# Fourier mixing and a gated FFN on one core: the odd item of the third stage goes ninth, and the first batch's loads, stores and conversions are put in another order

## The chip, the cores and the metric

The kernel runs on one core of a Trainium2 chip. The metric is the device time of one execution in microseconds (us). Before the change it is 2895.74 us, the median of three runs (2893.91 to 2896.57). A core has TensorE (PE, matmuls), VectorE (DVE), ScalarE (ACT), GpSimd (POOL) and SyncE (SP). In this kernel SP does nothing but issue DMA transfers; POOL issues DMA transfers too, and ACT issues the stores of the third stage. Each engine works through its own list of instructions strictly in the order in which they were written, so an instruction that waits holds up all that stand behind it on the same engine.

## The reference

Eight batches of 3072 rows by 256 channels go through a spectral mixing layer: a real Fourier transform along the rows, a complex 256x256 product at each frequency with a bias, a soft threshold, and the transform back. The result goes row by row through a feed-forward network of width 2048 with the activation h·tanh(softplus(h)). Weights of the network come as 64-bit floats.

```python
X = np.fft.rfft(x, axis=1)
Yr = Xr @ w_r - Xi @ w_i + b_r
Yi = Xr @ w_i + Xi @ w_r + b_i
Yr = np.sign(Yr) * np.maximum(np.abs(Yr) - lam, 0.0)      # the same for Yi
y = np.fft.irfft(Yr + 1j * Yi, n=3072, axis=1)
h = y @ w_in
out = (h * np.tanh(np.where(h > 20.0, h, np.log1p(np.exp(h))))) @ w_out
```

## The kernel before

Every product is done with operands that are split in a rounded high part ("hi") and the remainder ("lo"); three matmuls (hi·hi, lo·hi, hi·lo) stand for one. The split costs one instruction for hi (ACT's L197 in the first batch, DVE's L195 later) and one on DVE for lo (L198).

**The four stages of a batch.** The transform of 3072 points is factored. Stage one (`item_a`, 7 items, PE line L361, in the chain's segment 0) loads x and does 24-point transforms; its results go to a DRAM scratch s1 (store L380 in the first batch). Stage two (segment 1) alternates 12 blocks `item_b` (L427 and L430 in the first batch; the load of s1 is L398, the twiddle table "tt" is loaded at L406) with 12 mixing items `item_m` (L543 in the first batch), which add the bias, apply the threshold (DVE lines L481 to L483, output tile y) and store y to the scratch s3 (L572: four stores of 32 rows per block; the odd block 11 uses L562, L564 and L586). Stage three (`item_c`, PE L634) gathers lines of s3 by strided DMA loads (L612), and stores to the scratch s2 from ACT's queue (L637). It has 13 items: items 0 to 11 take 4 loads each, the odd item 12, which has the leftover frequencies, takes 6, and stands first. Stage four (`item_f`, PE L675 and L676, load of s2 at L652, its table vt at L657 from c_v in the first batch and at L659 from v_scr later) gives a piece of the rows y that the network reads. Two of its items make one chunk of 512 rows; a batch has six chunks.

**The network.** For each chunk, 16 steps of `ffn1` (L757: 6 matmuls of 128x512, then the activation on ACT at L762), `split_g` (L771, L772) and `ffn2` (L788: 12 matmuls of 128x256 per step).

**What sets the order.** The program is written out step by step by Python generators. `run_chain` walks through a batch's four segments; it issues the loads of the first `ahead_n` items of a segment before the segment starts, and then one item's loads ahead of each item (`ahead`). For the first batch `ahead_n` is 6 and nothing else fills PE, so the four stages run one after the other. After that, the network's steps of batch b run, and each step draws one piece of the chain of batch b+1 (`gen`, ahead_n 3) or of the next chunk's stage-four item (`extra`), whichever is there; `extra` goes first. So PE has, in each step, 6 + 12 matmuls of the network and one piece of a chain, and the loads of both chains stand in the one list of SP.

**The weight conversions.** The 16 pieces ("jobs") of the 64-bit weights are loaded from POOL (L261, tile raw, 512 KB each) and turned into float32 hi and lo by nine instructions each: seven on DVE (L269 to L285; the last comes with ACT's L287) and two (L291, L293) that finish the job inside the next one. `aux_steps(n)` writes the next n of these instructions. PACE gives how many of them follow one piece of segment 0, 1, 2 or 3 of the first batch; `on_seg` writes some between segments. At most 97 are written before the network starts; the rest follow in its first 19 steps. A raw tile is loaded as early as its place in POOL's list and its buffer allow.

**Queues.** In the first batch SP issues the loads of x, half of stage three's loads (those with g = 0) and all y stores; POOL issues tables, raw weights, bias, the constant uu of stage three, and the other half of stage three's loads (g = 1). From the second batch on, SP issues all loads and y stores. y tiles come from a pool of two (`p_z`), tables tt and vt from a pool of four (`p_t`).

Of the kernel before, what the change touches and what calls it, by code (L numbers as in the profile page):

```python
# [127 lines left out]
def fft_mix_ffn_kernel(ctx: ExitStack, tc: tile.TileContext, x, w_r, w_i, b_r, b_i, w_in, w_out,  # L128
                       c_fa, c_t0, c_t, c_u, c_v, out):
    nc = tc.nc  # L130
# [36 lines left out]
    started = [False]  # L167
# [128 lines left out]
    N_EARLY = 11  # L296
# [201 lines left out]
    def item_m(b, blk, src):  # L498
        it = Item()
# [56 lines left out]
        def store():  # L556
            y = it.y
            s3 = scratch(b)[1]
            yv = y.rearrange("p (s c) -> p s c", s=2)
            half = SEQ // 4  # L560
            if blk == 11:
                nc.sync.dma_start(out=s3[half, 1:2, :], in_=yv[0:1, 0, :])  # L562
                for h in range(2):
                    nc.sync.dma_start(  # L564
                        out=s3[0:half].rearrange("(i r) s c -> r i s c", r=12)[6 * h].rearrange("i s c -> i (s c)"),
                        in_=y[64 * h:64 * h + 64])
                return
            for e in range(2):
                for d in range(2):
                    r, x = (23 - blk, 1 - e) if d else (blk + 1, e)  # L570
                    rows = s3[(r % 2) * (half + 1):][0:half].rearrange("(i r) s c -> r i (s c)", r=24)
                    nc.sync.dma_start(out=rows[r // 2 + 12 * x], in_=y[64 * e + 32 * d:64 * e + 32 * d + 32])  # L572

        def nyq():
            xh, xl = src.x
# [68 lines left out]
    def item_f(b, nb):  # L644
        it = Item()
# [6 lines left out]
            nc.sync.dma_start(out=it.t, in_=s2[:, 2 * nb:2 * nb + 2, :].rearrange("q m c -> q (m c)"))  # L652

        def cload():
            it.v = p_t.tile([128, 2, 2, 128], F32R, tag="t", name="vt")
            if b == 0:
                nc.gpsimd.dma_start(out=it.v, in_=c_v[nb])  # L657
            else:
                nc.sync.dma_start(out=f32(it.v), in_=v_scr[nb])  # L659
# [30 lines left out]
    def chain(b):  # L690
        segs = [[item_a(b, p) for p in range(7)]]
        bm = []
        order = [11] + list(range(11))
        bs = [item_b(b, k) for k in order]
        for k in range(12):
            bm.append(bs[k])
            if k:
                bm.append(item_m(b, order[k - 1], bs[k - 1]))
        bm.append(item_m(b, order[11], bs[11]))
        segs.append(bm)  # L700
        segs.append([item_c(b, p) for p in (12, *range(12))])
        segs.append([item_f(b, 0), item_f(b, 1)])
        return segs

# [98 lines left out]
    with tc.manual_schedule():  # L803
# [9 lines left out]
        def aux_run():  # L813
            for n, job in enumerate(aux):
                aux_load(n + 1)
                for k, _ in enumerate(job.work(aux[n - 1] if n else None)):
                    if k == 5:
                        aux_load(n + (4 if n + 3 <= N_EARLY else 3))
                    yield
            yield from aux[-1].finish()  # L820

# [9 lines left out]
        def on_seg(k):  # L831
            if k == 1:
                setup_mix()
                aux_steps(4)
            elif k == 2:
                aux_steps(9)
            elif k == 3:
                aux_steps(8)

        PACE = (0.8, 0.9, 2.2, 2)  # L840
        first = chain(0)
        cnt = 0
        owed = 0.0
        for k in run_chain(first, ahead_n=6, ahead_a=3, cla=3, on_seg=on_seg):
            cnt += 1
            if cnt == 2:
                load_mix()
                aux_load(1)
            if cnt == 3:
                for it in first[1][:3]:  # L850
                    it.cload()
            if cnt == 5:
                load_bias()
                aux_load(2)
            if cnt == 9:
                aux_load(4)
            if cnt == 16:
                setup_u()
            if cnt > 5:
                owed += PACE[k]  # L860
            while owed >= 1:
                aux_steps(1)
# [71 lines left out]
```

## Time and profile before

| | before |
|---|---|
| median of three runs | 2895.74 us (2893.91 to 2896.57) |
| the profiled execution | 2898.05 us |
| its span, first to last instruction | 2896.3 us |
| mean granted TensorE clock | 0.981 |
| PE / DVE / ACT busy | 96% / 65% / 33% |
| DMA, mean over the span | 94 GB/s |

A row of the trace gives start, duration, engine, line, operation, output and input tiles and, in brackets, how long the engine had been idle before it and what ended that. "x4" at the end means four instructions that the answer merged; their time is the sum, so a merged row of a DMA queue runs from the first issue to the end of the last. The SP and POOL rows are issues; the transfer itself goes on after them. A row of stages gives, for a stretch of the span, the busy time of each engine with its number of instructions, the granted TensorE clock (1.00 is full), and the DMA's share and rate.

### The profile page before, as it was taken

How to read it: one execution, taken by the hardware profiler on the slowest of the kernel's cores; microseconds unless marked ns; L12 is line 12 of the kernel's file. 1: busy time of each engine (PE TensorE's matmuls, PEld its weight loads, DVE VectorE, ACT ScalarE, POOL GpSimd, SP SyncE). 2: the span in 40 equal slices, each digit the busy share in tenths (PEclk: the TensorE clock that was granted, in tenths of full speed). 3: DMA queues.
4: the chain of work that ended last, by engine and by line, in shares of the span. 5: the costliest groups of instructions: out<-in, count | busy, mean ns of one | idle time of the engine just before them, and what ended most of it. 6: DMA issues, size and time to landing. Idle time of an engine off the chain costs nothing.

```text
span 2896.3 us, 44966 instructions
## 1 busy us (share of the span) xinstructions
PE 2788.0 (96%) x17812; PEld 2506.2 (87%) x17812; DVE 1891.3 (65%) x3116; ACT 946.3 (33%) x1844; POOL 49.3 (2%) x90
## 2 busy tenths in 40 slices
PE   6779999999999999999999999999999999999999
PEld 4558988899898998889988899888989899889998
DVE  5888765767657775567755777567765777654443
ACT  3333333233333332333323333323333333232222
POOL 1210000000000000000000000000000000000000
PEclk9879999999999999999999999999999999999999
DMA  7654424232233322242233322432324232221010
GB/s 213 186 150 123 128 83 121 82 97 89 74 101 115 94 74 87 85 130 80 66 103 100 101 83 64 123 94 88 93 68 125 83 103 86 73 89 44 23 37 15
DMA packets 171528, 273.13 MB, mean 94 GB/s; under 512 B 22902, under 2 KB 67974, under 8 KB 170934
## 3 DMA queue, kind: packets, MB, share of 16 engines
q1 hardware_dynamic: 147958, 224.23, 25.7%
q10 hardware_dynamic: 13856, 25.17, 3.0%
q0 software_dynamic: 9504, 20.86, 2.6%
q8 instruction: 140, 2.29, 0.3%
q14 instruction: 70, 0.57, 0.1%
HBM read 169.49 MB, written 107.23 MB: 96 GB/s over the span
## 4 chain that ended last, share of the span: by engine, by line
PE 89%; DMA 4%; DVE 3%; SPq 2%; issue 1%; ACT 0%; POOL 0%; ACTq 0%; DVEq 0%; POOLq 0%
PE acc L788 37%; PE hp L757 35%; PE psp L526 4%; PE psa L361 2%; PE psc L634 2%; PE psk L507 2%; PE psf L675 2%; PE psb L442 2%; SPq L612 1%; PE psf L676 1%; PE psb L444 1%; DMA s<-y 1%; DMA lds<-s 1%; DVE lo L198 1%; DMA lds<-in_x_dram 0%
## 5 line engine op out<-in xcount | busy, mean ns | idle before, releaser
L788 PE MATMUL acc<-wout,gh 128*128 128x256 f32 x6144 | 1148.5, 285 | 0.0
L757 PE MATMUL hp<-yh,win 128*128 128x512 f32 x3072 | 1090.3, 395 | 5.0 <-ACT yh L684 4.3
L788 PEld LDWEIGHTS acc<-wout,gh 128*128 128x128 f32 x6144 | 977.7, 190 | 41.6 <-issue 6.0
L762 ACT ACTIVATE s<-hp 128x512 f32<-128x512 f32 x768 | 459.5, 598 | 1447.2 <-PE hp L757 1335.9
L788 PE MATMUL acc<-wout,gl 128*128 128x256 f32 x3072 | 871.1, 284 | 0.0
L757 PEld LDWEIGHTS hp<-yh,win 128*128 128x128 f32 x3072 | 582.1, 189 | 105.1 <-ACT yh L684 4.5
L757 PE MATMUL hp<-yl,win 128*128 128x512 f32 x1536 | 606.8, 395 | 0.0
L788 PEld LDWEIGHTS acc<-wout,gl 128*128 128x128 f32 x3072 | 583.8, 190 | 0.0
L772 DVE TENSOR_TENSOR gl<-s,gh 128x1024 fp32r<-128x1024 f32 x384 | 470.6, 1225 | 79.9 <-PE acc L788 42.6
L771 DVE CAST gh<-s 128x1024 fp32r<-128x1024 f32 x376 | 259.1, 689 | 332.8 <-ACT s L762 332.8
L757 PEld LDWEIGHTS hp<-yl,win 128*128 128x128 f32 x1536 | 291.0, 189 | 36.2 <-DVE yl L685 0.4
L198 DVE TENSOR_TENSOR lo<-ld,hi 120x512 fp32r<-120x512 f32 (+3 forms) x390 | 269.7, 692 | 28.9 <-ACT hi L197 16.3
L195 DVE CAST hi<-ld 120x512 fp32r<-120x512 f32 (+2 forms) x367 | 154.1, 420 | 82.6 <-DMA ld<-s 82.6
L679 DVE TENSOR_TENSOR eo<-psf,cor 128x256 f32<-128x256 f32 x192 | 77.3, 422 | 156.9 <-ACT cor L678 156.2
L634 PE MATMUL psc<-hi,uu 120*120 120x512 f32 (+1 forms) x224 | 93.0, 428 | 50.1 <-DVE hi L195 34.4
L526 PE MATMUL psp<-wmix,xh 128*128 128x256 f32 x672 | 133.0, 281 | 0.0
L361 PE MATMUL psa<-hi,fa 120*120 120x512 f32 (+1 forms) x224 | 97.2, 437 | 22.0 <-ACT hi L197 9.7
L526 PEld LDWEIGHTS psp<-wmix,xh 128*128 128x128 f32 x672 | 108.9, 188 | 3.7
L685 DVE TENSOR_TENSOR yl<-yt,yh 128x512 fp32r<-128x512 f32 x96 | 66.5, 693 | 67.0 <-ACT yh L684 67.0
L675 PE MATMUL psf<-vt,hi 128*128 128x256 f32 x384 | 95.3, 325 | 13.2 <-ACT hi L197 11.5
L684 ACT ACTIVATE yh<-yt 128x512 fp32r<-128x512 f32 x96 | 60.7, 632 | 139.4 <-DVE yt L682 139.4
L481 DVE TENSOR_TENSOR y<-psp,y 128x512 f32<-128x512 f32 x84 | 58.1, 691 | 70.3 <-PE psp L526 68.9
(107 smaller groups left out, 2419.4 us busy)
## 6 DMA issues: line engine op xcount, KB each, us to landing
ld<-s SPq DMA_DIRECT2D x185, 256.0 KB
out_dram<-ot SPq DMA_DIRECT2D x48, 512.0 KB
s<-y SPq DMA_DIRECT2D x352, 64.0 KB
ld<-in_x_dram SPq DMA_DIRECT2D x90, 240.0 KB
vt<-v_scr SPq DMA_DIRECT2D x84, 256.0 KB
s<-ev ACTq DMA_DIRECT2D x89, 240.0 KB
ld<-s SPq DMA_DIRECT2D x350, 60.0 KB
s<-eva SPq DMA_DIRECT2D x84, 240.0 KB
```

What stands on the lines that cost most here:

```text
L195: nc.vector.tensor_copy(out=hi, in_=src)
L198: nc.vector.tensor_tensor(out=lo, in0=src, in1=f32(hi), op=ALU.subtract)
L361: nc.tensor.matmul(out=ps[:K], lhsT=fa[:K, h, s, col:col + K], rhs=m[:K], start=n == 0, stop=n == 2)
L526: nc.tensor.matmul(out=it.ps[:, ri * 256:(ri + 1) * 256], lhsT=m[:, c, 130 - ri * 128:258 - ri * 128], rhs=wmix[:, c, s, 2 * ri, :], start ...
L634: nc.tensor.matmul(out=ps[:K, sl], lhsT=uu[:K, var, s, :K], rhs=m[:K, sl], start=n == 0, stop=n == 2)
L675: nc.tensor.matmul(out=ps[:, p], lhsT=it.hi[:, q:q + 128], rhs=it.v[:, p], start=True, stop=False)
L679: nc.vector.tensor_tensor(out=eo[:, c], in0=ps[:, :, 0], in1=cor, op=ALU.add)
L757: nc.tensor.matmul(out=hp, lhsT=win[:, k, s, f * 128:(f + 1) * 128], rhs=m[:, k, :], start=n == 0, stop=n == 5)
L762: nc.scalar.activation(out=s_t[t // 2][:, t % 2, :], in_=hp, func=ACTF.Mish)
L771: nc.vector.tensor_copy(out=gh, in_=s)
L772: nc.vector.tensor_tensor(out=gl, in0=s, in1=f32(gh), op=ALU.subtract)
L788: nc.tensor.matmul(out=p, lhsT=m[:, t % 2, o:o + 128], rhs=wout[:, f, s, :], start=f == 0 and h == 0 and n == 0, stop=last and h == 1 and ...
```

## The change

The change has two parts. The first acts in every batch: stage three's items run in the order 0 to 7, 12, 8 to 11, so the item with six loads stands ninth. The second acts in the first batch alone:

- the y stores with d = 1 (two of the four of a block, 22 in all) are issued from POOL and no longer from SP;
- the two tables vt of the first stage-four items are written after the 57th piece (in stage three) and no longer at the start of segment 3; `cload` returns at once where the table is there;
- `load_mix` (four transfers on SP) moves from the second to the seventh piece, behind all loads of x; the bias loads from the fifth to the seventh in the program; the first three stage-two tables from the third to the eleventh; uu from the 16th to the 20th;
- conversions: 12 instead of 9 before stage three, 10 instead of 8 before stage four; PACE 1.6 instead of 0.8 in stage one, 1.6 instead of 2.2 in stage three, and counting starts one piece earlier. The total before the network stays 97;
- before the network has started, no raw load beyond the twelfth is written.

```diff
@@ item_m, store
-                    nc.sync.dma_start(out=rows[r // 2 + 12 * x], in_=y[64 * e + 32 * d:64 * e + 32 * d + 32])
+                    (nc.gpsimd if d and b == 0 else nc.sync).dma_start(out=rows[r // 2 + 12 * x], in_=y[64 * e + 32 * d:64 * e + 32 * d + 32])
@@ item_f
         def cload():
+            if hasattr(it, "v"):
+                return
             it.v = p_t.tile([128, 2, 2, 128], F32R, tag="t", name="vt")
@@ chain
-        segs.append([item_c(b, p) for p in (12, *range(12))])
+        segs.append([item_c(b, p) for p in (*range(8), 12, *range(8, 12))])
@@ aux_run
-                        aux_load(n + (4 if n + 3 <= N_EARLY else 3))
+                        aux_load(min(n + (4 if n + 3 <= N_EARLY else 3), 16 if started[0] else N_EARLY + 1))
@@ on_seg
-                aux_steps(9)
+                aux_steps(12)
             elif k == 3:
-                aux_steps(8)
-
-        PACE = (0.8, 0.9, 2.2, 2)
+                aux_steps(10)
+
+        PACE = (1.6, 0.9, 1.6, 2)
@@ the loop over the first batch
-            if cnt == 2:
+            if cnt in (2, 5, 9):
+                aux_load(1 + (cnt > 2) + 2 * (cnt > 5))
+            if cnt == 7:
                 load_mix()
-                aux_load(1)
-            if cnt == 3:
+                load_bias()
+            if cnt == 11:
                 for it in first[1][:3]:
                     it.cload()
-            if cnt == 5:
-                load_bias()
-                aux_load(2)
-            if cnt == 9:
-                aux_load(4)
-            if cnt == 16:
+            if cnt == 20:
                 setup_u()
-            if cnt > 5:
+            if cnt == 57:
+                for it in first[3]:
+                    it.cload()
+            if cnt > 4:
                 owed += PACE[k]
```

How the order moves on two engines, at three places. First SP, at the start of stage three of the second batch (s_1444 is that batch's scratch s3, s_166 the first batch's scratch s2, whose loads are those of stage four). Before:

```order
L572 DMA s_1444<-y 32x512 x12
L612 DMA ld<-s_1444 48x1x256 x2
L612 DMA ld<-s_1444 36x1x256 x2
L612 DMA ld<-s_1444 12x1x256 x2
L612 DMA ld<-s_1444 60x1x256 x8
L652 DMA ld<-s_166 128x1x512
L796 DMA out_dram<-ot 128x2x512
L612 DMA ld<-s_1444 60x1x256 x4
L652 DMA ld<-s_166 128x1x512
L612 DMA ld<-s_1444 60x1x256 x36
```

The same place with the change:

```order
L572 DMA s_1444<-y 32x512 x12
L612 DMA ld<-s_1444 60x1x256 x12
L652 DMA ld<-s_166 128x1x512
L798 DMA out_dram<-ot 128x2x512
L612 DMA ld<-s_1444 60x1x256 x4
L652 DMA ld<-s_166 128x1x512
L612 DMA ld<-s_1444 60x1x256 x16
L612 DMA ld<-s_1444 48x1x256 x2
L612 DMA ld<-s_1444 36x1x256 x2
L612 DMA ld<-s_1444 12x1x256 x2
L612 DMA ld<-s_1444 60x1x256 x16
```

Ahead of the first stage-four load stand 12 gathering loads where 14 stood, and the odd item's six come 20 loads later, behind the second stage-four load. The later batches have the same pieces.

Second, POOL in stage two of the first batch (tt are the tables of the blocks, s_165 is the scratch s3). Before:

```order
L213 DMA uu<-in_c_u_dram 120x720
L261 DMA raw<-in_moe_w_out_dram 128x2x512
L406 DMA tt<-in_c_t_dram 128x512 x4
L261 DMA raw<-in_moe_w_out_dram 128x2x512
L406 DMA tt<-in_c_t_dram 128x512 x3
L261 DMA raw<-in_moe_w_in_dram 128x1024
L406 DMA tt<-in_c_t_dram 128x512 x2
L261 DMA raw<-in_moe_w_in_dram 128x1024
```

With the change:

```order
L406 DMA tt<-in_c_t_dram 128x512 x2
L261 DMA raw<-in_moe_w_out_dram 128x2x512
L406 DMA tt<-in_c_t_dram 128x512
L213 DMA uu<-in_c_u_dram 120x720
L572 DMA s_165<-y 32x512 x2
L406 DMA tt<-in_c_t_dram 128x512
L572 DMA s_165<-y 32x512 x2
L406 DMA tt<-in_c_t_dram 128x512
L572 DMA s_165<-y 32x512 x2
L261 DMA raw<-in_moe_w_in_dram 128x1024
L406 DMA tt<-in_c_t_dram 128x512
L572 DMA s_165<-y 32x512 x2
```

The sixth raw tile and uu now come before the first y store; from then on each table stands behind a pair of y stores, which wait for DVE, and two of the tables also stand behind a raw load (the piece shows one of the two).

Third, POOL between stages three and four of the first batch. Before:

```order
L612 DMA lds<-s_165 60x1x256 x2
L612 DMA ld<-s_165 60x1x256 x2
L261 DMA raw<-in_moe_w_in_dram 128x1024 x2
L657 DMA vt<-in_c_v_dram 128x512 x2
L261 DMA raw<-in_moe_w_out_dram 128x2x512 x2
```

With the change:

```order
L612 DMA lds<-s_165 60x1x256 x2
L612 DMA ld<-s_165 60x1x256 x2
L659 DMA vt<-in_c_v_dram 128x512 x2
L261 DMA raw<-in_moe_w_in_dram 128x1024
L261 DMA raw<-in_moe_w_out_dram 128x2x512 x2
```

The tables vt stand ahead of the last early raw load, and only one such load is left behind stage three's loads; the other one has moved up among them. On DVE, 14 conversion instructions now stand ahead of the last stage-one sum (L374) and not 6, 12 of them between the last y of stage two and stage three rather than 9 (each time with one more that the pace adds), and 9 rather than 15 stand between the last stage-four instruction and the first `split_g` of the network.

## The prediction

> **What bounds the kernel now.** I read the page first, then a table of the start by stage, then PE's waits after it.
>
> ```profile
> span 2896.3 us, 44966 instructions
> PE 2788.0 (96%) x17812; PEld 2506.2 (87%) x17812; DVE 1891.3 (65%) x3116; ACT 946.3 (33%) x1844; POOL 49.3 (2%) x90
> ```
>
> PE is busy for 2788.0 of 2896.3 us, so 108.3 us are idle. The change neither adds nor removes a matmul, so apart from the clock it can win only where PE stands still. The table of the start, in stages cut at PE's gaps:
>
> ```profile
> 0.00:41.40 41.40, 24.43 (x42) 10.41 (x42) 18.49 (x32) 13.02 (x21) 7.54 (x17) 1.00 0.94 259
> 49.70:107.80 58.10, 56.55 (x294) 48.11 (x294) 49.48 (x93) 16.00 (x31) 6.59 (x12) 1.00 0.55 157
> 107.80:117.50 9.70, 0.00 (x0) 0.00 (x0) 7.21 (x14) 1.73 (x3) 5.95 (x11) 0.64 0.42 107
> 117.50:146.20 28.70, 21.39 (x42) 9.85 (x42) 20.39 (x38) 14.53 (x26) 12.57 (x22) 0.62 0.79 236
> 146.20:157.60 11.40, 0.00 (x0) 0.00 (x0) 6.60 (x13) 2.38 (x4) 1.26 (x3) 0.50 0.67 200
> 166.20:250.00 83.80, 75.75 (x398) 62.38 (x399) 75.48 (x130) 32.48 (x54) 6.22 (x10) 0.92 0.46 130
> ```
>
> The columns are span, PE, PE's weight loads, DVE, ACT, POOL, clock, DMA share, GB/s. Stage one is bound by DMA (share 0.94), stage two by PE and DVE alike (56.55 and 49.48 of 58.10). Then come two gaps without a matmul, 9.70 us before stage three and 11.40 us before stage four, and a start of the network in which DVE (75.48) is as busy as PE (75.75). After that PE has one kind of wait left worth naming. First its group from 240 us to 2900, then all seven places:
>
> ```profile
> PE psc L634 <- DVE hi L195: 34.4, 7, 6.2
> ```
>
> ```profile
> 435.17 0.53 PE L634 MATMUL psc<-hi,uu 96*96 96x256 f32 x1 [4.00 <-DVE hi L195]
> 782.13 0.53 PE L634 MATMUL psc<-hi,uu 96*96 96x256 f32 x1 [4.48 <-DVE hi L195]
> 1129.86 0.53 PE L634 MATMUL psc<-hi,uu 96*96 96x256 f32 x1 [6.23 <-DVE hi L195]
> 1476.69 0.53 PE L634 MATMUL psc<-hi,uu 96*96 96x256 f32 x1 [5.14 <-DVE hi L195]
> 1823.87 0.39 PE L634 MATMUL psc<-hi,uu 96*96 96x256 f32 x1 [4.91 <-DVE hi L195]
> 2171.29 0.53 PE L634 MATMUL psc<-hi,uu 96*96 96x256 f32 x1 [4.70 <-DVE hi L195]
> 2517.69 0.53 PE L634 MATMUL psc<-hi,uu 96*96 96x256 f32 x1 [4.90 <-DVE hi L195]
> ```
>
> Once in each later batch, PE stops 4.0 to 6.2 us before the first item of stage three. What DVE waits for stands on SP's list; the timeline of the first of these places, SP and then DVE:
>
> ```profile
> 419.18 10.92 SPq L612 DMA_DIRECT2D ld<-s  x14
> 430.14 0.56 SPq L652 DMA_DIRECT2D ld<-s  x1
> ```
>
> ```profile
> 433.62 0.43 DVE L195 CAST hi<-ld 128x512 fp32r<-128x512 f32 x1 [8.24 <-DMA ld<-s]
> 434.70 0.42 DVE L195 CAST hi<-ld 96x512 fp32r<-96x512 f32 x1
> ```
>
> SP issues the 14 gathering loads of the odd item and of items 0 and 1 in one run, and only then, at 430.14, the load of the network's next stage-four item (L652). DVE must split that one (128x512, at 433.62) before it may split stage three's first item (96x512), whose data are long there. So PE waits for a place in SP's list.
>
> **The change, part by part.** *The odd item, all batches.* Twelve loads now stand ahead of L652. The six of the odd item and four of a plain one, from SP's timeline in short pieces:
>
> ```profile
> 423.74 0.79 SPq L612 DMA_DIRECT2D ld<-s  x1
> 426.98 0.75 SPq L612 DMA_DIRECT2D ld<-s  x1
> ```
>
> The odd item takes 419.18 to 423.74, 4.56 us; item 0 takes 423.74 to 426.98, 3.24; item 1 the rest to 430.14, 3.16. Three plain items take about 9.54 us where 10.96 went by, so L652 is issued 1.42 us earlier, and DVE's split and PE's restart follow: 7 x 1.42 = 9.9 us. Each gap stays longer than that (4.00 is the shortest), so nothing else ends the wait first. The six loads ninth cost nothing by my reading: they add 1.4 us to SP's list in a run of single items, and DVE waits for none of their loads there; without that cover they would cost up to the same 1.4 us a batch.
>
> Part of it goes back through the clock. PE restarts slowly; the granted clock behind the stop, and a group of 12 L788 matmuls there and before the stop (from its first row to the next group's first):
>
> ```profile
> 435.00:441.00 6.00, 5.64 (x22) 5.06 (x23) 4.69 (x8) 0.59 (x1) 0.00 (x0) 0.50 0.36 108
> ```
>
> ```profile
> 428.18 0.40 PE L788 MATMUL acc<-wout,gh 128*128 128x256 f32 x2
> 429.62 0.40 PE L757 MATMUL hp<-yh,win 128*128 128x512 f32 x1
> ...
> 437.07 0.63 PE L788 MATMUL acc<-wout,gh 128*128 128x256 f32 x2
> 439.63 0.63 PE L757 MATMUL hp<-yh,win 128*128 128x512 f32 x1
> ```
>
> At clock 0.50 the group takes 2.56 us, not 1.44: 44% of such time is lost. If the slow stretch ends when it ended before, 44% of the time won is spent in it: 4.4 us of 9.9 at the most; if it moves with the restart, none. I take +1.5, as several stretches begin near the restart. Term: -8.4 (from -9.9 to -5.5).
>
> *Stage one.* Twice as many conversions follow each piece, so 14 stand before the last sum and not 6. DVE from the split of the eighth x tile to that sum:
>
> ```profile
> 27.98:43.33 15.35, 11.22 (x21) 5.13 (x21) 12.91 (x24) 7.56 (x14) 0.00 (x0) 1.00 0.84 277
> ```
>
> A conversion instruction costs 6.60/13 = 0.51 us (stage table, the gap before stage four). Eight more make 12.91 + 4.1 = 17.0 us of DVE in a stretch of 15.35: +1.7 us, because DVE takes the bound from the DMA. The weight loads behind all of x and uu out of the way speed x up, which can at best use up DVE's waits (2.44). I take +1.5 (from -2.4 to +1.7).
>
> *Stage two.* The sixth raw load goes out before the first y store and no longer beside it. DVE's first wait for a y buffer and the chain's step behind it:
>
> ```profile
> 67.50 0.69 DVE L481 TENSOR_TENSOR y<-psm,bias 128x512 f32<-128x512 f32 x1 [1.52 <-DMA s<-y]
> ```
>
> That wait should go: -1.5 (0 if the store stays slow). Against it, each table now waits on POOL behind two y stores. A table load's landing between 40 and 110 us, its issue, the end of one y, and the block that uses the table:
>
> ```profile
> L406 POOL DMA_DIRECT2D tt<-in_c_t_dram x9: 528/531/551, 53.0 to 85.0; - x9
> DMA to landing us min/median/max: 2.9/3.3/4.6
> 94.47 0.69 DVE L483 TENSOR_TENSOR y<-y,cl 128x512 f32<-128x512 f32 x1
> 100.16 0.33 PE L430 MATMUL psb<-tt,hi 128*128 128x128 f32 x2
> ```
>
> The y ends at 95.16, its table's block starts at 100.16: 5.0 us. A store on POOL is unseen; the nearest issue is 0.53, so two take 1.06, the table lands 3.3 later, and 0.6 is left. Two tables also stand behind a raw load; its landing from 55 to 160 us:
>
> ```profile
> DMA to landing us min/median/max: 4.8/5.7/6.9
> ```
>
> These come 1.06 + 0.55 + 5.7 - 5.0 = 2.3 us late each. PE runs a little ahead of DVE here, which hides part: +1.5 for both (0 to +4.6). Who waits is PE's block and then DVE's sums.
>
> [...]
>
> *Stage three.* Three more conversions before it (1.5 us) lie in DVE's idle time, 9.70 - 7.21 = 2.49. Inside it, 0.6 x 13 x 0.51 = 4.0 us of DVE go, but DVE is busy for only 20.39 of 28.70: -0.5 (-2 to 0). The last y stores on two queues save issue time on SP, and I give nothing for it.
>
> *Before stage four.* POOL's issues, and three steps from the chain of waits:
>
> ```profile
> 145.84 0.56 POOL L261 DMA_DIRECT2D raw<-in_moe_w_in_dram  x1 [12.97 <-DVE win L293]
> 146.38 1.08 POOL L657 DMA_DIRECT2D vt<-in_c_v_dram  x2
> ```
>
> ```profile
> 108.31 2.39 DMA s<-y
> 147.78 5.75 DMA s<-ev
> 153.86 3.08 DMA lds<-s
> ```
>
> The last store of stage three, issued at 147.78, lands only after 5.75 us, because 1 MB (one raw, two vt) went out just before it. Now vt and that raw load go earlier; the store then takes about the 2.39 us of a y store: -3.3. It cannot be more than DVE's idle time in the gap, 11.40 - 6.60 = 4.8, and is 0 if the next raw load takes the place.
>
> *Start of the network.* 9 conversions, not 15, stand before the first `split_g`: 3.1 us of DVE. PE's gap there:
>
> ```profile
> 177.80 0.49 PE L361 MATMUL psa<-hi,fa 120*120 120x512 f32 x1 [2.83 <-DVE hi L195]
> ```
>
> It should all but go: -2.7 (-3.1 to 0). The six were moved to stage one, where they were charged above.
>
> **Sum.** -8.4 + 1.5 - 1.5 + 1.5 - 0.5 - 3.3 - 2.7 = -13.4. The profiled execution took 2898.05 us, 1.75 of it around the span, so it becomes 2884.6; it lies 2.31 above the runs' median, so the median becomes **2882.3**.
>
> **Rivals.** *The start wins nothing* (0.12): raw loads keep POOL's list and the DMA as full as before, so tables come late (+4.6), y's buffer wait stays (0), the store before stage four stays slow (0). With -8.4 + 1.5 - 0.5 - 2.7 that is -5.5, 2890.2, at the edge of no change. For it: two raws stand ahead of tables. Against: fewer bytes stand behind stage three.
>
> *The clock holds* (0.11): the slow stretch does not follow a shorter stop. After the change the stops would be 2.6, 3.1, 4.8, 3.7, 3.5, 3.3 and 3.5 us. If three escape and each loses no 44% of some 5.7 us (435.17 to 441, as far as the slow rows go), 7.5 us more are won: 2874.8; all seven give 2864.8. Against: the stop of 2.83 us at 177.80 is followed by a 512-wide matmul of 0.49 us, where one at full clock took 0.40 (429.62). [...]
>
> *Slower* (0.04): the tables, queued behind y stores, pace stage two. If they land like the slowest raw load (6.9), five are 1.06 + 6.9 - 5.0 = 3.0 us late and two, behind a raw, 6.8: 28.6 us in place of +1.5 gives +13.7, 2909. It decides the sign once seven tables are 2.1 us late on average, a landing of 6.1; the slowest of nine took 4.6.
>
> *The stop is not SP's* (0.05): the odd item's loads ninth, or another load, take its place; only the start's -5.0 stays, 2890.7.
>
> **How the numbers follow.** The forecast has 0.68. Its own range, from the bounds that can fall together, is 2875 to 2889. Taking in part of the clock's case below and of the start's case above gives 2871 to 2892 for 8 in 10. A change under 0.2% (5.8 us, 2889.9 to 2901.5) cannot be told from none. Faster: 0.68 + 0.11 and about half of the start's case, 0.85; the same 0.11; slower 0.04.
>
> **What would show it.** Right: seven stops before L634 of about 3.5 us (24 to 25 us in total), with 12 L612 ahead of L652; vt issued near 133 us and the store before stage four landing in about 2.4 us; stage one's last sum a little later than 43.3. Wrong: stops unchanged in length, a new PE wait near the ninth item or on tt, or a slow stretch missing after the stops.

## The result, and the profile after

The changed kernel takes 2875.98 us (median of four runs, 2873.03 to 2877.48) where the kernel before takes 2896.15 us beside it. The ratio is 0.9929, with a 95% interval of 0.9912 to 0.9946: 20 us faster. The forecast was 2882.3 us, in a range of 2875 to 2889. The profiled execution took 2874.97 us; its page begins:

```profile
span 2873.1 us, 44977 instructions
PE 2779.6 (97%) x17812; PEld 2497.7 (87%) x17812; DVE 1891.6 (66%) x3116; ACT 946.0 (33%) x1844; POOL 60.4 (2%) x112
```

PE is busy for 8.4 us less with the same 17812 matmuls, so part of the gain is clock and not idle time. (Lines behind L655 are two higher than before: L757 is L759, L788 is L790, L675 is L677.)

**The later batches.** SP's list at the first of the seven places, PE's waits after 240 us in total, and three of the seven stops:

```profile
410.97 10.04 SPq L612 DMA_DIRECT2D ld<-s  x12
421.05 0.56 SPq L652 DMA_DIRECT2D ld<-s  x1
```

```profile
PE psc L634 <- DVE hi L195: 24.1, 7, 4.2
```

```profile
426.28 0.50 PE L634 MATMUL psc<-hi,uu 120*120 120x512 f32 x1 [2.87 <-DVE hi L195]
...
1460.86 0.49 PE L634 MATMUL psc<-hi,uu 120*120 120x512 f32 x1 [3.31 <-DVE hi L195]
...
2495.25 0.49 PE L634 MATMUL psc<-hi,uu 120*120 120x512 f32 x1 [3.24 <-DVE hi L195]
```

The stops fell from 34.4 to 24.1 us in total. The last restart came at 2517.69 before and comes at 2495.25 now, 22.4 us earlier. It splits so: the first stop begins at 426.28 - 2.87 = 423.41 and not at 435.17 - 4.00 = 431.17, so the start gave 7.8 us; the first stop is 1.1 shorter; the six batches from the first restart to the last take 2068.97 us for 2082.52, 13.55 less. The six stops in them account for 30.36 - 21.22 = 9.1 of that; the other 4.4 must be matmuls that ran faster. The clock record bears this out: in those six batches PE is busy at half clock for 31.4 us before and 22.0 with the change, and 44% (the prediction's loss at half clock) of the 9.4 us between them is 4.1. The clock around the second and the third stop:

```profile
770.00:773.40 3.40, 3.34 (x11) 2.68 (x12) 3.23 (x6) 0.60 (x1) 0.00 (x0) 0.50 0.19 54
773.40:776.80 3.40, 3.40 (x25) 3.15 (x25) 1.75 (x4) 1.26 (x3) 0.00 (x0) 1.00 0.86 259
...
1115.20:1118.60 3.40, 3.37 (x11) 2.71 (x12) 3.25 (x5) 0.60 (x1) 0.00 (x0) 0.50 0.20 54
1118.60:1122.00 3.40, 3.40 (x14) 2.92 (x13) 1.33 (x3) 0.00 (x0) 0.00 (x0) 0.57 0.85 261
```

Behind the stop at 770 the clock is half for one stretch of 3.41 us, behind the one at 1115 for two. In the trace's clock record there were seven stretches of 6.83 us before (47.8 us); now there are none behind the first stop, four of 3.41 and two of 6.83 (27.3 us).

**The start**, in the stages of the prediction's first table, of the changed kernel:

```profile
49.31:103.95 54.64, 53.00 (x294) 45.29 (x294) 49.64 (x93) 15.92 (x31) 17.84 (x34) 1.00 0.65 183
103.95:113.51 9.56, 0.00 (x0) 0.00 (x0) 8.55 (x18) 1.66 (x3) 7.58 (x14) 0.70 0.51 133
113.51:143.04 29.53, 23.34 (x42) 10.25 (x42) 17.92 (x32) 14.53 (x26) 12.67 (x23) 0.50 0.82 239
143.04:150.16 7.12, 0.00 (x1) 0.01 (x1) 6.51 (x14) 1.89 (x4) 0.73 (x1) 0.50 0.55 168
```

Stage two begins 0.4 us earlier and is 3.4 shorter, stage three is 0.9 longer, the gap before stage four falls from 11.45 to 7.12. Of these, the runs below show only the gap to be the change's work.

### The profile page after: what moved, and what is told of

It reads as the page before. It is cut to its first block, busy times and chain, and to the rows that moved or that the text cites. A ratio compares the mean times of both kernels' runs of the same rounds, so it can differ in the third digit from the quotient of the medians.

```text
span 2873.1 us, 44977 instructions
## 1 busy us (share of the span) xinstructions
PE 2779.6 (97%) x17812; PEld 2497.7 (87%) x17812; DVE 1891.6 (66%) x3116; ACT 946.0 (33%) x1844; POOL 60.4 (2%) x112
## 4 chain that ended last, share of the span: by engine, by line
PE 89%; DMA 4%; DVE 3%; SPq 2%; issue 1%; ACT 1%; POOL 0%; ACTq 0%; DVEq 0%
PE acc L790 37%; PE hp L759 35%; PE psp L526 4%; PE psc L634 2%; PE psa L361 2%; SPq L612 2%; PE psk L507 2%; PE psf L677 2%; PE psb L442 2%; DMA ld<-s 1%; DMA lds<-in_x_dram 1%; PE psf L678 1%; PE psb L444 1%; DVE lo L198 1%; PE psb L427 0%
## 5 line engine op out<-in xcount | busy, mean ns | idle before, releaser
L790 PE MATMUL acc<-wout,gh 128*128 128x256 f32 x6144 | 1145.7, 284 | 0.0
L759 PE MATMUL hp<-yh,win 128*128 128x512 f32 x3072 | 1089.5, 395 | 5.2 <-ACT yh L686 4.6
L790 PEld LDWEIGHTS acc<-wout,gh 128*128 128x128 f32 x6144 | 975.4, 189 | 42.0 <-issue 6.0
L790 PE MATMUL acc<-wout,gl 128*128 128x256 f32 x3072 | 870.1, 283 | 0.0
L759 PEld LDWEIGHTS hp<-yh,win 128*128 128x128 f32 x3072 | 581.8, 189 | 105.1 <-ACT yh L686 4.8
L759 PE MATMUL hp<-yl,win 128*128 128x512 f32 x1536 | 606.5, 395 | 0.0
L790 PEld LDWEIGHTS acc<-wout,gl 128*128 128x128 f32 x3072 | 582.3, 190 | 0.0
L759 PEld LDWEIGHTS hp<-yl,win 128*128 128x128 f32 x1536 | 290.8, 189 | 36.3 <-DVE yl L687 0.4
L198 DVE TENSOR_TENSOR lo<-ld,hi 120x512 fp32r<-120x512 f32 (+3 forms) x390 | 269.8, 692 | 29.6 <-ACT hi L197 16.9
L634 PE MATMUL psc<-hi,uu 120*120 120x512 f32 (+1 forms) x224 | 91.6, 423 | 39.6 <-DVE hi L195 24.1
L361 PE MATMUL psa<-hi,fa 120*120 120x512 f32 (+1 forms) x224 | 96.3, 436 | 19.2 <-DMA fa<-in_c_fa_dram 7.2
L374 DVE TENSOR_TENSOR eva<-psa,s2nd 120x512 f32<-120x512 f32 (+1 forms) x112 | 72.9, 685 | 47.1 <-ACT s2nd L366 27.4
```

The costliest lines, as they stand in the source:

```text
L198: nc.vector.tensor_tensor(out=lo, in0=src, in1=f32(hi), op=ALU.subtract)
L361: nc.tensor.matmul(out=ps[:K], lhsT=fa[:K, h, s, col:col + K], rhs=m[:K], start=n == 0, stop=n == 2)
L374: nc.vector.tensor_tensor(out=evv[e][:K], in0=it.ps[:K].rearrange("p (j c) -> p j c", j=2), in1=s2nd[:K].rearrange("p (j c) -> p j c", j=2 ...
L634: nc.tensor.matmul(out=ps[:K, sl], lhsT=uu[:K, var, s, :K], rhs=m[:K, sl], start=n == 0, stop=n == 2)
L759: nc.tensor.matmul(out=hp, lhsT=win[:, k, s, f * 128:(f + 1) * 128], rhs=m[:, k, :], start=n == 0, stop=n == 5)
L790: nc.tensor.matmul(out=p, lhsT=m[:, t % 2, o:o + 128], rhs=wout[:, f, s, :], start=f == 0 and h == 0 and n == 0, stop=last and h == 1 and ...
```

## The experiments

Two things were open: whose the 4.4 us of clock are, and which edit of the start did what. Each kernel was timed against the kernel before on the same chip (2895 to 2898 us there).

**The odd item alone, and the start alone.** The first is the kernel before with one line:

```diff
-        segs.append([item_c(b, p) for p in (12, *range(12))])
+        segs.append([item_c(b, p) for p in (*range(8), 12, *range(8, 12))])
```

> The kernel before with one line of the change: the odd item ninth. Theory A (the batches' gain belongs to this line alone): the seven stops before the first L634 fall from 34.4 us in total to 24 or 25, the half-clock stretches behind them from 47.8 us to some 27, and the time by 15.4 us, to about 2880.5. Theory B (my prediction's clock term was right, and the changed kernel's shorter half-clock stretches are an accident of its shifted start): stops 24 to 25 us, but seven stretches of 6.8 us stay, and the time falls by 8.4 to 9.9 us, to about 2887.

The second is the changed kernel with that line put back.

> The changed kernel with the odd item first again, so only the start's edits are left. Theory A: the seven stops stay at 34 us in total, the stretches at 47.8 us, and the time falls by the 7.8 us that the first stop comes earlier, to about 2888. Theory B (the phase of the clock's windows at each stop decides, and a shift of the start changes it): stops 34 us, but some stretches of 3.4 us in place of 6.8, and 3 to 6 us more are won, 2882 to 2885.

The odd item alone: 2881.21 us, ratio 0.9946 (0.9934 to 0.9958), -15.6 us (-12 to -19). The start alone: 2893.07 us, ratio 0.9987 (0.9978 to 0.9995), -3.8 us (-1.4 to -6.4). Together that is -19.4, so the two parts add up to the change. PE's waits after 240 us, of the first kernel and then of the second:

```profile
PE psc L634 <- DVE hi L195: 23.4, 7, 4.3
```

```profile
PE psc L634 <- DVE hi L195: 34.3, 7, 5.6
```

Theory A of the first run holds: with the old start, too, six of the seven stretches are one window of 3.41 us, and one is 6.83. The second run has the shifted start with the long stops, and there six stretches of 6.83 us and one of 3.41 remain. So the shorter half-clock time belongs to the shorter stops and not to the shifted start. The time of the second run missed both theories, 7.8 us and more: that figure came from two single executions, and the start is worth about half of it in the medians.

**Eight loads ahead of L652.** In the changed kernel's `run_chain`, the third item's four loads are written behind the four pauses that precede stage three, in later batches only:

```diff
-            while at[0] < min(n, la):
+            while at[0] < min(n, la - (1 if gap and k == 2 else 0)):
                 seg[at[0]].load()
                 at[0] += 1
...
                 yield None
+            while at[0] < min(n, la):
+                seg[at[0]].load()
+                at[0] += 1
             while at[2] < min(n, pla):
```

> The changed kernel, with the third item's four loads in the later batches issued only after the two pauses in which the network's next stage-four load L652 goes out: 8 of L612 stand ahead of L652, not 12. Theory A (SP's list is the stop): L652 goes out 3.2 us earlier, the stops of 3.2 to 4.2 us fall to under 1 us each and the half-clock stretches vanish. That gives 24.1 - 3 = 21 us of stops and some 44% of 27.3 us, 12 us: about 2843. Rival (another load, or the split before it, is next in line): the stops keep over 2 us each, or a wait of the same size shows before the third item, whose loads now come later; then no more than 10 us are won, 2866 or above.

2842.69 us, ratio 0.9814 (0.9802 to 0.9827): 33 us better than the change, and 54 better than before. SP's list, and the waits that are left:

```profile
411.62 6.49 SPq L612 DMA_DIRECT2D ld<-s  x8
418.49 0.57 SPq L652 DMA_DIRECT2D ld<-s  x1
```

```profile
PE psc L634 <- DVE hi L195: 3.0, 4, 2.0
```

One stop of 2.0 us is left, and no half-clock stretch between 240 us and the last microseconds of the program. A batch, from first L634 to first L634, takes 339.5 to 340.2 us where PE does not stop and the clock stays full. That is the floor against which the others can be priced: 347.1 on average before (5.1 stop, 2.0 clock), 344.8 with the change (3.5 stop, 1.3 clock). The third item's loads are now issued 8 us after the first two items' (419.76 for 411.62), and no wait of PE names them.

**The same edit in the kernel before**, odd item first, which leaves 10 loads ahead:

> The kernel before, odd item first, with only the third item's four loads in the later batches put behind the four pauses: 10 of L612 ahead of L652, not 14. By SP's list L652 goes out 3.16 us earlier, and the stops become 0.8, 1.3, 3.1, 2.0, 1.8, 1.5 and 1.7, 12 us for 34.4. Theory A (the clock answers only stops of more than about 2.5 us): at most one or two half-clock stretches of 3.4 us are left, 18 to 19.5 us more won; -40 to -42, about 2856. Theory B (it answers each stop over 1 us): six or seven stretches of 3.4 us stay, about 10.5 us won; -32.6, about 2864. If the odd item's place mattered by itself, the stops would stay near 4 us and the time above 2880.

2869.71 us (2862.16 to 2874.26), ratio 0.9910 (0.9894 to 0.9925). The list explains the stops to the tenth:

```profile
PE psc L634 <- DVE hi L195: 11.9, 7, 2.4
```

The expected total was 12. Where L652 stands decides; the odd item's own place does not, since a batch without stretch and less its stop takes 339.9 to 340.3 us here, with the odd item first, as in the kernel above with it ninth. The clock fits neither theory: two stretches in the profiled execution, behind stops of 2.18 and 2.42 us, but executions up to 12 us slower beside it. So the same kernel was profiled twice more. The second time:

> The kernel before with the third item's loads late, profiled a second time. Its first four executions took 2862 to 2874 us at granted clocks of 0.987 and 0.982 to 0.983, and the first profile (the 0.987 one) showed two half-clock stretches of 3.4 us behind stops of 2.2 and 2.4 us. Theory (the same stop may or may not be followed by a stretch, by chance of where it falls): the stops are again 1 to 2.5 us, but a slower execution shows four or more stretches behind them. Rival (the stretches follow from the stops' lengths): again two, and a slower execution is slow elsewhere, in its start.

It took 2860.46 us, with stops of 11.2 us in total and two stretches. Three stops of it:

```profile
1115.59 0.36 PE L634 MATMUL psc<-hi,uu 96*96 96x256 f32 x1 [2.26 <-DVE hi L195]
...
1798.29 0.36 PE L634 MATMUL psc<-hi,uu 96*96 96x256 f32 x1 [1.92 <-DVE hi L195]
...
2140.06 0.36 PE L634 MATMUL psc<-hi,uu 96*96 96x256 f32 x1 [1.69 <-DVE hi L195]
```

Of these three only the shortest, 1.69 us, was followed by a stretch; the other stretch stands behind the longest stop, 2.61 us. Length alone does not decide. A slower execution was not caught here, so the theory's four or more stretches stayed untried.

**The change, profiled again**, for the same question:

> The changed kernel, profiled a second time. Theory: stops before L634 again 23 to 25 us in total; stage two 54.6 us or 58 to 59, by the moment at which PE comes to full speed; the half-clock stretches 24 to 34 us in total, not behind the same stops as in the first profile.

2875.95 us, stops 23.4 us in total, stretches 30.7 us. Two stops of nearly equal length, and PE in the windows around them:

```profile
1463.64 0.78 PE L634 MATMUL psc<-hi,uu 120*120 120x512 f32 x1 [2.71 <-DVE hi L195]
...
1808.62 0.49 PE L634 MATMUL psc<-hi,uu 120*120 120x512 f32 x1 [2.74 <-DVE hi L195]
```

```profile
1459.34:1462.75 3.41, 1.58 (x8) 0.97 (x6) 0.62 (x2) 0.60 (x1) 0.00 (x0) 1.00 0.87 308
1462.75:1466.16 3.41, 2.52 (x7) 1.87 (x8) 3.24 (x7) 0.55 (x1) 0.00 (x0) 0.53 0.13 38
1466.16:1469.57 3.41, 3.41 (x14) 3.09 (x13) 2.18 (x3) 0.05 (x1) 0.00 (x0) 0.50 0.70 197
...
1804.08:1807.49 3.41, 1.80 (x10) 1.18 (x8) 0.42 (x1) 0.60 (x1) 0.00 (x0) 1.00 0.85 304
1807.49:1810.91 3.42, 2.06 (x12) 1.66 (x13) 3.32 (x7) 0.60 (x1) 0.00 (x0) 1.00 0.15 46
```

The first stop is followed by 6.83 us at half clock, the second by none. The windows are cut on a grid that the clock record itself gives: after 240 us, all changes of the clock of one execution lie a multiple of 3.413 us apart. In the first window of the first stop PE is busy 1.58 of 3.41 us, less than half, and the clock halves; in the second stop's two windows it is busy 1.80 and 2.06, more than half, and nothing happens. The stop at 1463 fills most of one window, the stop at 1808 is cut in two by a grid point. The rule was fitted on 13 profiles, with two numbers (the share, and 0.2 us by which the window ends ahead of the grid point), and then tried on a new one:

> The kernel before with the third item's loads late, profiled a third time, to try a rule that the traces so far suggest. In 13 profiles all changes of the granted clock between 240 and 2700 us lie on a grid of 3.413 us; the clock halves where matmuls filled less than 0.50 of the 3.413 us that ended 0.2 us before a grid point, and not otherwise (539 grid points near stops of over 0.7 us, 65 halvings, no exception), and it comes back where they filled some 0.9. Theory: the same holds for this new trace's seven stops of 0.8 to 2.6 us without exception; a stop under 1.7 us that stands alone is never followed by a stretch, one of 1.7 to 3.4 is by the luck of the grid, in s/3.41 of the cases. Rival (the fit is chance, or a length decides): at least one of the stops breaks it.

The rule held at all of that trace's grid points, two halvings among them. Two cases of it:

```profile
1116.38:1119.79 3.41, 1.47 (x7) 0.86 (x5) 0.65 (x2) 0.60 (x1) 0.00 (x0) 1.00 0.89 321
1119.79:1123.21 3.42, 2.37 (x10) 2.08 (x11) 3.25 (x7) 0.42 (x1) 0.00 (x0) 0.53 0.27 79
...
2143.79:2147.20 3.41, 1.72 (x9) 1.10 (x7) 1.47 (x4) 0.60 (x1) 0.00 (x0) 1.00 0.77 272
2147.20:2150.62 3.42, 3.05 (x21) 2.77 (x22) 3.28 (x5) 0.60 (x1) 0.00 (x0) 1.00 0.36 99
```

1.47 of 3.41 us (0.43): halved. 1.72 of 3.41 (0.502 by the trace's unrounded times): not. The other halving of that trace came at 0.497. This execution took 2866.81 us, 6.3 more than the one before it. It had 10.2 us of stretches after 240 us for 6.8; half of the difference, 3.3 us, is its stage two (58.00 us for 54.68), which the next runs explain.

**Stage two, and the kernel before a second time.**

> The kernel before, profiled a second time, for its stage two. Theory (the 58.04 us of stage two in the first profile are an accident: PE came to full speed only 9.7 us after the stage's first matmul, where the changed kernel needed 4.1): another execution gives a length between 54.6 and 58.9 us that follows the moment at which 512-wide matmuls of L543 go from 0.63 us for a middle one to 0.39. Rival (the edits of stage two made the 3.4 us): 58.0 us again within 0.3 whatever that moment is.

2898.92 us, with a stage two of 58.85 us. The clock came back 9.2 us after the stage's first matmul, earlier than in the first profile, and yet the stage was longer, by a wait of 2.48 us for a y buffer (1.52 in the first profile). So this run decides for neither theory. Next, the changed kernel with all y stores on SP again:

```diff
-                    (nc.gpsimd if d and b == 0 else nc.sync).dma_start(out=rows[r // 2 + 12 * x], in_=y[64 * e + 32 * d:64 * e + 32 * d + 32])
+                    nc.sync.dma_start(out=rows[r // 2 + 12 * x], in_=y[64 * e + 32 * d:64 * e + 32 * d + 32])
```

> The changed kernel with all y stores of the first batch on SP again. Theory A (stage two won 3.4 us because the sixth raw load no longer runs beside the first y stores): the wait for a y buffer stays away, stage two stays at 54.7 us or gets 1 us shorter, as the two waits for tables (1.6 us) go; time within 2 us of the changed kernel's, about 2875. Rival (it was the second queue): the wait for a y buffer returns with 1.5 us or more, stage two goes back to 57 to 58 us and the time to about 2879.

2875.91 us, ratio 0.9931 (0.9919 to 0.9942): in the time, the stores' queue makes no difference that shows. But its profile has a stage two of 58.87 us and a wait for a y buffer of 2.3 us, so neither theory holds whole. Single 512-wide matmuls early in that stage in the kernel before (first profile), and then one in the changed kernel:

```profile
57.00 0.63 PE L543 MATMUL psm<-wmix,xl 128*128 128x512 f32 x1
...
59.48 0.39 PE L543 MATMUL psm<-wmix,xl 128*128 128x512 f32 x1
```

```profile
54.31 0.39 PE L543 MATMUL psm<-wmix,xl 128*128 128x512 f32 x1
```

All 14 profiles begin stage two, behind a gap of 8 to 10 us, at half speed (in the change four 256-wide matmuls take 1.05 us there and 0.64 later). What differs is how long that lasts. In the table, the second column is the time from the stage's first matmul to the clock record's return to full, where the matmuls change their pace too. The third is the share that matmuls fill of the 3.41 us window in which the stage begins, with the grid carried back from the later changes of the same trace:

| profile | half speed lasts, us | first window filled | stage two, us |
|---|---|---|---|
| before, twice; third item late, third profile | 9.7, 9.2; 9.2 | 0.77, 0.63; 0.64 | 58.05, 58.85; 58.00 |
| stores on SP; old pace (below) | 9.9; 9.7 | 0.85; 0.77 | 58.87; 58.01 |
| odd item alone; third item late, first two profiles | 4.7; 3.5, 4.0 | 0.32; 0.00, 0.12 | 54.67; 54.09, 54.68 |
| change, twice; start alone; eight ahead | 3.8, 3.9; 3.9; 3.7 | 0.07, 0.07; 0.08; 0.03 | 54.64, 55.31; 55.57; 54.64 |
| without the early vt; steps moved (both below) | 3.8; 4.3 | 0.06; 0.20 | 54.91; 55.58 |

The old start stands on both sides, three long and three short, so stage two's 3.4 us in the first comparison can't be put down to an edit. Whether the edits shift the odds is open: the six profiles with the new bursts and the second queue are all short, and the two that take one of these back are long. What goes with the length in all 14 profiles is where the grid cuts the stage's start: the long phase has a first window filled to 0.63 or more, the short one to 0.32 or less. No run set this, it is read from the traces. The wait for a y buffer comes with it: 1.5 to 2.5 us where the half speed is long and the stores are on SP, 0.4 to 0.7 us where it is short and the stores are on SP, and none in the profiles with the second queue.

**The pace of the conversions.** The changed kernel with the old numbers:

```diff
-                aux_steps(12)
+                aux_steps(9)
...
-                aux_steps(10)
+                aux_steps(8)
...
-        PACE = (1.6, 0.9, 1.6, 2)
+        PACE = (0.8, 0.9, 2.2, 2)
...
-            if cnt > 4:
+            if cnt > 5:
```

> The changed kernel with the old pace of the conversion steps. My term for the start of the network says: 15 conversions again stand before the first split_g, PE's gap of 1.83 us there grows back to about 2.8 and the gap behind the fourth stage's tiles with it, 2 to 3 us later in all; my term for stage one says: the last sum L374 and stage two come some 1.5 us earlier. Together 0 to +1.5 us, about 2877. Rival (the work moved into stage one was free, and the network's start pays in full): +2.7 to +3.1, about 2879.

2878.72 us, ratio 0.9936 (0.9923 to 0.9948): not to be told from the change, whose interval covers it. Stage by stage it is another matter. Stage two begins, stage four begins, and the network's first L361 follows at:

```profile
46.06 0.58 PE L427 MATMUL psb<-tt,hi 128*128 128x256 f32 x1 [8.42 <-ACT hi L197]
...
153.11 0.58 PE L677 MATMUL psf<-vt,hi 128*128 128x256 f32 x1 [10.81 <-ACT hi L197]
...
173.27 0.49 PE L361 MATMUL psa<-hi,fa 120*120 120x512 f32 x1 [2.90 <-DVE hi L195]
```

Stage two begins 3.25 us earlier than with the new pace (49.31), and that is lost again: 3.7 us in the gap before stage four (10.81 for 7.12) and 1.1 in PE's gap at the network's start (2.90 for 1.83). Neither theory fits: the time came near the rival's, but the profiled execution has the long stage two, 58.01 us, some 3.4 more than the change's, and by the table that need not be the edit's work.

**The early vt and the limit on raw loads**, taken out of the changed kernel:

```diff
-                        aux_load(min(n + (4 if n + 3 <= N_EARLY else 3), 16 if started[0] else N_EARLY + 1))
+                        aux_load(n + (4 if n + 3 <= N_EARLY else 3))
...
-            if cnt == 57:
-                for it in first[3]:
-                    it.cload()
```

> The changed kernel without the early vt and without the limit on raw loads: 1 MB stands in front of stage three's last store again. Theory (my term before stage four): that store lands after 5 to 6 us, PE's gap before stage four goes from 7.1 back to about 11 us, and the time rises by 3.3 to 4.3 us, to about 2880. Rival (the raw loads are out of the way already through the earlier start, or the gap is made of DVE's conversions): the gap stays under 8.5 us, time within 1.5 us of the changed kernel's 2876.

2874.52 us, ratio 0.9923 (0.9910 to 0.9935), and the gap stays. POOL's issues in it, and stage four's first matmul:

```profile
135.40 0.57 POOL L261 DMA_DIRECT2D raw<-in_moe_w_in_dram  x1 [6.56 <-DVE win L293]
135.97 1.20 POOL L659 DMA_DIRECT2D vt<-in_c_v_dram  x2
...
149.85 0.58 PE L677 MATMUL psf<-vt,hi 128*128 128x256 f32 x1 [7.15 <-ACT hi L197]
```

The rival was right. The raw load waits for DVE to finish a piece of the conversions, and vt stands behind it; with the new pace it goes out at 135.40, 8 us ahead of the last store (143.37), and not 1.9 us ahead of it as before (145.84 and 147.78), so 1 MB is out of the store's way. In the run with the old pace vt was early, but the raw load went out at 142.41, 1.95 us ahead of the store (144.36), and the load behind that store could only be issued at 149.28, 4.9 us later; with the change it is 143.70 and 146.33, 2.6 us. The pace does it; on top of it the early vt and the limit do nothing that shows. With the old pace the early vt may give a little: the gap of 10.81 us stands against 11.4 to 12.6 in the six profiles of kernels with the old start.

**Both gains of the pace at once?** On top of the eight loads ahead, the old pace in stage one and in stage three, with the new bursts of 12 and 10 steps kept:

> The kernel with eight loads ahead of L652 (2842.7 us), and in it eight of the first batch's conversion steps moved out of stage one into stage three: the old pace in both, the longer bursts before stages three and four kept. Theory (stage one's first 46 us are DVE's, and the old pace there gave stage two's first matmul at 46.06 us; the gap of 7.1 us before stage four belongs to the longer bursts, which let the raw load go out 7 us before the last store): stage two begins 3 us earlier, the gap stays near 7, stage three grows by 0 to 1.5, time 2839.5 to 2841. Rival (the steps moved into stage three put the raw load beside the last store again, as in the run with the whole old pace): the gap goes to 10 or 11, time 2843 to 2845.

2843.20 us, ratio 0.9811 (0.9798 to 0.9824), the same as without. Its stage three and the gap before stage four:

```profile
111.37:143.34 31.97, 22.91 (x42) 10.32 (x42) 21.17 (x38) 15.04 (x27) 13.61 (x24) 0.50 0.78 222
143.34:151.57 8.23, 0.00 (x1) 0.01 (x1) 7.27 (x16) 1.90 (x4) 0.71 (x1) 0.50 0.60 202
```

Stage two began at 46.01 us, 3.9 earlier. Stage three paid 2.6 of it back (29.41 in the kernel without this edit) and the gap 1.1. The time is the rival's, but its reason holds only in part: the raw load went out at 140.10, between the two cases. The longer stage three is not the time of DVE's own steps: PE's three longest stops in it (1.71, 3.26 and 3.03 us) end with ACT's split of a gathered load, and DVE stood idle before its own part of the same splits for 1.62, 3.09 and 3.21 us. The run with the whole old pace has as many steps per piece in its stage three, and that took 28.66 us. Why it grew here stays open. In both runs, what the old pace won in stage one was lost again before the network.

## Why the prediction was right in sign and 6 us short

- **What bounds the kernel, and the odd item's stops**: right. The term was -9.9 us; the stops lost 10.3. SP's list up to L652 is shorter by 8.8 us of it over the seven places (at the first, 12 loads took 10.04 us, where the prediction's three plain items were to take 9.54). And SP's list alone gave the totals of other kernels beforehand: 24 to 25 us with 12 loads ahead (23.4 measured), 12 with 10 (11.9), 3 with 8 (3.0).
- **"Part of it goes back through the clock", +1.5**: this is the step that failed. In the first comparison the clock gave 4.4 us in six batches, and some 5 with the seventh, in place of taking 1.5; the order alone brought 15.6 us where -8.4 stood. The working assumed that a stretch ends when it ended before or moves with the restart, whole. It does neither: a stretch is one or two windows of 3.41 us, and a shorter stop mostly leaves one. The 44% was too high as a price of stretch time, too: a stretch cost 2.0 us a batch before, 30% of 6.83, in part because 1.3 of the 6.83 us, on average, lie inside the stop itself.
- **"The clock holds" (0.11)**: half right. Its total for three escapes, 2874.8, lies nearer to the measured time than the forecast does, but not for its reason. No run shows that three of the seven should escape: one stop did, four kept a stretch of 3.41 us and two one of 6.83. The argument against it misread a row: the 512-wide matmul of 0.49 us behind the stop of 2.83 us is no sign of half clock, since the first one behind a stop takes 0.50 us at full clock too (426.28 above, where no stretch follows) and 0.78 at half (1463.64 above). The conclusion stands by the clock record, which has a stretch of 3.41 us from about 1 us after that restart. The stop's length alone does not decide: 1.69 us was followed by half clock in one place, 2.87 us not in another.
- **Stage one, +1.5**: the balance was nothing that shows, since stage two begins at 49.1 to 49.7 us in the profiles with the old start and at 49.0 to 50.1 in those with the new one and the new pace. The parts were larger. With the new order of loads and the old pace, stage two begins at 46.06, so in single profiles the loads gave 3.65 us (49.71 - 46.06) and the new pace took 3.25. The last sum, expected a little later, ends 0.4 us earlier.
- **Stage two, -1.5 and +1.5**: about right in sum. The 3.4 us can't be put down to the change; among the short stages two the new start's are 0 to 1.5 us longer. The late tables came as forecast, 1.6 us of waits for tt in two places, and they are absent with the stores on SP. The y buffer's wait goes with the clock at the stage's start.
- **Stage three, -0.5**: 0.9 longer in the first comparison, which is within its spread (28.4 to 29.9 us with the old start, 27.4 to 29.6 with the new start and the new pace).
- **Before stage four, -3.3**: measured 4.3 in the gap. The mechanism (loads issued just in front of the last store) was right, but one raw load of 512 KB is enough for most of it, as the run with the old pace shows; and it was put down to the early vt and the limit, and the pace does it.
- **Start of the network, -2.7**: the gap fell by 1.0 us only (2.83 to 1.83), though the profiles agree on it: 2.6 to 2.9 with the old pace, 1.83 or 1.84 with the new bursts of 12 and 10 steps.
- **The start's sum, -5.0**: right, but by luck, as too much hoped for at the network's start and feared in stage one was made up before stage four. Between executions with the same kind of stage two, the first stop begins at 423.4 and 424.1 us in the two profiles of the change, and at 428.3 to 429.4 in the three of old-start kernels with a short stage two, about 5 us later. In the medians the start alone gave 3.8 us (1.4 to 6.4).
- **Slower, by tables behind y stores**: no. POOL issued them in 565 ns at the median, little more than the 531 ns of before, with DVE busy 49.64 of stage two's 54.64 us and 22 stores more on that queue:

```profile
L406 POOL DMA_DIRECT2D tt<-in_c_t_dram x9: 536/565/690, 52.6 to 92.1; - x9
DMA to landing us min/median/max: 2.8/3.9/4.8
```

## What to carry to other kernels

When PE waits at the start of a stage, count what one queue must issue ahead of the load that is truly needed: here each pair of gathering loads costs 1.6 us, and moving four of them behind a pause was worth more than the whole change. Price a PE stop as idle time plus the half-clock stretch behind it (3.41 or 6.83 us here), and shorten it until it fills less than half a window of 3.413 us. (By the author's estimate from the same windows, filling a long stop with some matmuls in its middle should do as well; no run tried it.) Before a microsecond of a single profile is put down to an edit, profile the same kernel a second time.

## What the runs showed of the hardware

**The clock changed at points of a fixed grid.** In 14 profiles, between 240 and 2700 us, the granted clock halved 67 times, always at a point of the trace's 3.413 us grid. Each time matmuls had filled less than half of the 3.413 us that ended 0.2 us before (0.497 at most); at all other grid points with the clock at full they had filled 0.501 or more. It came back where they filled about 0.9 (0.91 and more in 66 of 67 cases, 0.89 in one; in the 29 windows after which it stayed at half, 0.90 at most). So of 86 stops of over 0.7 us, all 35 of more than 3.41 us were followed by half clock, 31 of the 40 between 1.7 and 3.41, by where they fell, and one of the 11 below: in its window the stop of 1.69 us had a second pause of 0.36 us beside it, and matmuls filled 1.45 of 3.42 us. So the same kernel has more or less half clock from one execution to the next: 6.8 and 10.2 us in two with the third item late, 27.3 and 30.7 us in two of the change. The rule is read from traces; no run set the phase of the grid.

**The record of the clock can miss a slow phase.** The rows give a granted clock of 1.00 for the change's whole stage two, and its first matmuls still run at half speed:

```profile
50.64 1.05 PE L427 MATMUL psb<-tt,hi 128*128 128x256 f32 x4
...
251.75 0.64 PE L427 MATMUL psb<-tt,hi 128*128 128x256 f32 x4
```

Four matmuls 256 wide take 1.05 us at 50.64 and 0.64 at 251.75; in the odd-item-alone run the same four take 1.05 us with the record at 0.50. The change's record has no entry before 53.16 us, where it begins with full clock, and the rows count the time before the first entry as 1.00. So the 1.00 of stage one in the prediction's table is no measurement either: the 512-wide matmuls of L361 take 0.63 to 0.78 us there, and 0.39 to 0.43 where a record that begins earlier (36.04 us, third item late, second profile) shows full clock. It also follows that mean granted clocks of executions can't be compared when their records begin at different times: that second profile has a mean of 0.984 with 2860.46 us, the first 0.987 with 2862.16.

**Not settled**: why the long phase at stage two's start lasts through one fully busy window more than the return rule above allows (five of five long cases, by the matmuls' pace). And why the kernel with 10 loads ahead had executions of 2871.57 and 2874.26 us: the slowest one that was profiled, 2866.81, is explained for the most part by its long stage two and one window of half clock more.
